# Attention moved whole ahead of the first MLP, in blocks of 32 queries by 38 keys, with a fixed TensorE order and weights kept on chip

## The chip, the core and the metric

One core of a Trainium2 chip runs the whole program. The engines are TensorE (PE; its weight loads are PEld), VectorE (DVE), ScalarE (ACT), GpSimd (POOL) and SyncE (SP), which here issues all DMAs. The metric is the device time of one execution in microseconds (us), lower is better, and the median of several runs is compared.

## What is computed

Attention of 2 batches, 8 heads, 576 positions and head size 64, a gated MLP (512 to 2048 to 512) and a dense MLP of four experts (512 to 1024 to 512), all in float32. Cut to what matters:

```python
out_d = sm_attn(q_d, k_d, v_d)             # q, k, v averaged over 4 neighbours: 144 positions
out_up = np.repeat(out_d, 4, axis=2)
mask = np.abs(pos[:, None] - pos[None, :]) < 4      # 7 keys for each query
attn = softmax(np.where(mask, scores, -1e9))
x = out_up + attn @ v                      # -> 1152 tokens x 512
h = x @ w_in                               # 512 x 2048, float64 in memory
g = h * np.clip(h + 3.0, 0.0, 6.0) / 6.0
x = g @ w_out                              # 2048 x 512, float64 in memory
for e in range(4):
    out += p[:, e:e+1] * (np.maximum(x @ w1[e], 0.0) @ w2[e])
```

## The kernel before

**MLP products.** Each float32 product runs as three float32r passes (function `three`, L246 to L248): every operand is split into a high and a low part, and high*high, high*low and low*high are added up in PSUM. So weights are needed as split tiles `whl` of 128 x 2 x 1024.

**Conversion.** The first MLP's weights are 16 float64 tiles (8 of `w_in`, even numbers; 8 of `w_out`, odd ones). The generator `converting()` turns each into float32 `cm` and splits it. For one tile DVE runs one L166 (mantissa), two L177 (low words), one L188 (power of two) and two L202 (product); ACT runs two L146 and two L155 (high part), and POOL two L156 (low part). Each `yield` is a step; the code that emits the kernel takes steps between other work. The float32 tile is also written to a DRAM buffer `kept` (L159).

**First MLP.** Tokens go in three blocks of 512, 352 and 288 (`BLOCKS`). For each of 16 pieces f of the hidden size `first(b, f)` makes 12 matmuls into PSUM `ps`, ACT (L584) and DVE (L586) make the gate `u`, ACT (L558) and DVE (L559) split it into `g`, and two pieces later `second(b, f)` makes 12 matmuls into the accumulators `acc`. `first` for an even f needs tile f, `second` tile f+1. For blocks 2 and 3 all 16 tiles are read back from `kept` and split again: DVE L227 copies the high part, DVE or POOL (L231) subtracts.

**Attention.** A pair of heads (128 partitions) and a chunk of 288 positions make three groups: each head's local part, in 3 tiles of 96 queries by 104 keys, and both heads' pooled part. A group goes through `scores` (L386 mask, L395 or L405 products, L414 maximum, L417), `exps` (L426, one ACT instruction for each tile, with its sum), `norm` (L438, L447, and POOL L448), `turn` (L463 transposes, L469 copy) and `values` (L481, L492, L500, L502, L510, L512: the split `x`). The local products use all 128 rows of the array, with zeros in the other head's half of `qz`. Chunks 0 and 1 stand ahead of the first MLP, chunk 2 is emitted between the pieces of block 1, chunk 3 between those of block 2.

**Order.** Each engine runs its own instructions in a fixed order and waits on semaphores. The code is written in emission order; a scheduler of the framework then orders each engine's list, TensorE's too.

**Second MLP.** For each expert and 384 tokens, `first2` (8 pieces of 12 matmuls of 384 columns; L655, L656 split) and then the second product (L778 to L780, 512 columns, L790).

Of the kernel before, what the change touches and what calls it, by code (L numbers as in the profile page):

```python
# [17 lines left out]
F32 = mybir.dt.float32  # L18
# [58 lines left out]
def model(ctx: ExitStack, tc: tile.TileContext, qT, kT, v, dp, w_in, w_out, w1, w2, out):  # L77
    nc = tc.nc
    const = ctx.enter_context(tc.tile_pool(name="const", bufs=1))
    big = ctx.enter_context(tc.tile_pool(name="big", bufs=1))  # L80
    rawp = ctx.enter_context(tc.tile_pool(name="raw", bufs=3))
    wa_p = ctx.enter_context(tc.tile_pool(name="wa", bufs=NWA))
    dram = ctx.enter_context(tc.tile_pool(name="kept", bufs=1, space=bass.MemoryType.DRAM))
    acc_p = ctx.enter_context(tc.tile_pool(name="accp", bufs=1, space=PSUM))
    mm_p = ctx.enter_context(tc.tile_pool(name="mm", bufs=2, space=PSUM))
    early_p = tc.alloc_tile_pool(name="early", bufs=1)
    att = tc.alloc_tile_pool(name="att", bufs=1, side="right")
    cv_p = tc.alloc_tile_pool(name="cv", bufs=2, side="right")
    sc_p = tc.alloc_tile_pool(name="sc", bufs=1, space=PSUM)

    products = [mm_p]

    def product():
        products.append(products.pop(0))
        return products[-1].tile([P, 512], F32, tag="mm", name="ps")

    def wide(i):
        return acc_p.tile([P, 512], F32, tag=f"acc{i}", name=f"acc{i}")

    EARLY = [lambda: sc_p.tile([P, 512], F32, tag="sc", name="sc")]  # L100
    EARLY += [lambda i=i: wide(i) for i in (0, 1, 3)]
    EARLY += [lambda: sc_p.tile([P, 512], F32, tag="tr", name="tr"), lambda: wide(2)]
    EARLY += [product]
# [5 lines left out]
    kept = [dram.tile([P, 2, WT], F32, name=f"kept{i}") for i in range(NW1 // 2)]  # L109
# [3 lines left out]
    for _ in BLOCKS[1:]:  # L113
        sources += [k.rearrange("p a n -> p (a n)") for k in kept]
# [4 lines left out]
    # Split tiles by number: 16 of the first MLP for each block, then 8 for each expert.  # L119
    first_e = NW1 * len(BLOCKS)  # L120
# [8 lines left out]
    def converting():  # L129
        """Rounds UP times the float64 tiles to float32, splits and keeps them. Yields at each step.  # L130

        The top 16 bits of a float64, as if they were a bfloat16, are a number whose exponent and
        mantissa hold float64's exponent. As a float16 they have its lower 8 bits, in float32's
        bias, where a bfloat16 has its exponent, so without the mantissa that is the power of two
        (tiny numbers vanish, huge ones saturate; REBIAS moves the range). It multiplies the
        mantissa, which is its upper 20 bits with the leading one, plus the low word over 2**32,
        and so 2**20 times what it stands for.
        """
# [11 lines left out]
        def put(i):  # L150
            f = m_t.pop(i)
            whl[i] = wa_p.tile([P, 2, WT], F32R, tag="w", name="whl")
# [10 lines left out]
        for i in range(NW1):  # L163
# [32 lines left out]
            if i:  # L196
                while i - 1 - NWA > used[0]:
                    yield True
                put(i - 1)
# [5 lines left out]
        while NW1 - 1 - NWA > used[0]:  # L205
            yield True
# [5 lines left out]
    split = [NW1]  # L212

    def split_to(n):
        """Splits up to tile n: the float32 tiles, after the converted ones."""
        while n >= 0 and n < NW1 and n not in whl and next(conv, 0) is None:
            pass
        while split[0] <= min(n, first_e + 8 * E - 1):
            i = split[0]
            j = NW1 + (i - NW1) // 2  # L220
            load_to(j)
            pool = pools["w1"] if i >= first_e and (i - first_e) % 8 < 4 else wa_p
            t = pool.tile([P, 2, WT], F32R, tag="w", name="whl")
            src = raw[j][:, (i % 2) * WT : (i % 2 + 1) * WT]
            for s in HALVES:
                if i < first_e:
                    nc.vector.tensor_copy(t[:, 0, s], src[:, s])  # L227
                else:
                    nc.scalar.activation(out=t[:, 0, s], in_=src[:, s], func=AF.Copy)  # L229
                eng = nc.gpsimd if i < first_e and i % 2 else nc.vector  # L230
                eng.tensor_tensor(  # L231
                    out=t[:, 1, s], in0=src[:, s], in1=r32(t[:, 0, s]), op=ALU.subtract
                )
            whl[i] = t
            split[0] += 1
            if i % 2:
                raw.pop(j)
                load_to(j + 3)

    pools = {}  # L240
# [10 lines left out]
    NQB = 5  # L251
    qz = [att.tile([P, 2, CH], F32, name=f"qz{i}") for i in range(NQB)]
    q_t, k_t, vw_t, vd_t, qd_t, kd_t = {}, {}, {}, {}, {}, {}

    def load_q(j):
        c, hp = divmod(j, NHP)
        b, s = divmod(c, 2)
        t = qz[j % NQB]
        nc.sync.dma_start(out=t[0:D, 0], in_=qT[b, s, 0:D, hp])
        nc.sync.dma_start(out=t[D:P, 1], in_=qT[b, s, D:P, hp])  # L260
        q_t[c, hp] = t

    def load_k(b, hp):
        t = att.tile([P, S], F32, tag="k", name="k", bufs=NHP)
        nc.sync.dma_start(out=t, in_=kT[b, :, hp])
        k_t[b, hp] = t

    def window(c, i):
        q0 = (c % 2) * CH + i * QT
        return min(max(q0 - (FACTOR - 1), 0), S - W)  # L270

    def load_v(c):
        for i in range(NQ):
            ks = window(c, i)
            t = att.tile([W, DM], F32, tag=f"vw{i}", name=f"vw{i}", bufs=2)
            nc.sync.dma_start(out=t, in_=v[c // 2, ks : ks + W, :])
            vw_t[c, i] = t
# [4 lines left out]
    vr_t = {}  # L282

    def load_vpool(b):
        for kc in range(2):
            t = wa_p.tile([P, 2, WT], F32R, tag="w", name="vr")
            t = r32(t[:KC]).rearrange("p a (r d) -> p (a r) d", r=2)
            nc.sync.dma_start(
                out=t,
                in_=v[b, kc * KC * FACTOR : (kc + 1) * KC * FACTOR, :].rearrange(  # L290
                    "(p r) d -> p r d", r=FACTOR
                ),
            )
            vr_t[b, kc] = t

    def pool_v(b, eng):
        vd_t[b] = att.tile([KC, 2, DM], F32, tag="vd", name="vd")
        for kc in range(2):
            t = vr_t.pop((b, kc))
            for r in range(2):  # L300
                add(eng, t[:, r], t[:, r], t[:, r + 2])
            add(eng, vd_t[b][:, kc], t[:, 0], t[:, 1])

    def sum4(src, n, tag, eng):
        """Sums of four neighbours of src [P, 4n]."""
        t = att.tile([P, n], F32, tag=tag, name=tag, bufs=NHP if tag == "kd" else 2)
# [4 lines left out]
        half = att.tile([P, n, 2], F32, tag="half", name="half", bufs=2)  # L311
# [5 lines left out]
    for i in range(4):  # L317
        load_k(0, i)
        load_q(i)
        if i == 1:  # L320
            load_v(0)
        if i == 2:
            load_vpool(0)
    load_q(NHP)
    load_v(1)
    warm = const.tile([P, 1], F32, name="warm")
    nc.vector.memset(warm, 0.0)
# [30 lines left out]
    class Group:  # L358
# [112 lines left out]
        def values(self):  # L471
            """Products with v, of the pair's three groups together."""
            aT_t[self.kind] = self.aT
            if self.kind < 2:
                return
# [375 lines left out]
```

## Time and profile before

| | |
|---|---|
| median of 3 runs | 745.77 us (745.34 to 747.49) |
| span of the profiled execution, first to last instruction | 741.5 us |
| busy: PE, PEld, DVE, ACT, POOL | 688.2, 619.5, 399.6, 243.3, 187.1 us |
| first product of MLP 1, first of MLP 2, last matmul | at 63.6, 334.4 and 738.1 us |

The profiled execution has only its span; the device time of a run has 4.3 us more around it (745.77 - 741.5). Instructions on PE are pipelined, so a busy PE is no proof of full speed.

### The profile page before, as it was taken

The numbers are of one execution on the slowest core, as the hardware profiler recorded it, in microseconds if no ns is written. First come the engines' busy times: TensorE is split into PE (matmuls) and PEld (weight loads), VectorE is DVE, ScalarE is ACT, GpSimd is POOL, SyncE is SP. The second block draws the span as 40 slices with busy tenths as digits, with TensorE's granted clock in tenths as the row PEclk, the third lists the DMA queues.
The fourth block names the chain that finished last, engine by engine and source line by source line (L and its number), as shares of the span: only waits on it lengthen the run. The fifth ranks groups of instructions, "written<-read, shape, count | busy, mean of one in ns | idle before, by whom it ended". The sixth has DMA issues, their size and how long they took to land.

```text
span 741.5 us, 10241 instructions
## 1 busy us (share of the span) xinstructions
PE 688.2 (93%) x3960; PEld 619.5 (84%) x3960; DVE 399.6 (54%) x754; ACT 243.3 (33%) x670; POOL 187.1 (25%) x163
## 2 busy tenths in 40 slices
PE   4967977788999899999999999999999999999998
PEld 4855765566898889989898989989898989989897
DVE  6998999999777768895121442223341223322121
ACT  3785545653343433264020431103230112201020
POOL 2688497795345344410000000000000000000000
PEclk9997998999999999999999999999999999999999
DMA  7855865565332233464000311001130000000001
GB/s 184 274 177 169 238 242 173 203 224 174 114 114 66 106 114 114 171 242 156 0 1 1 114 57 57 1 1 57 57 114 1 0 1 1 0 15 29 30 15 43
DMA packets 16301, 71.40 MB, mean 96 GB/s; under 512 B 2172, under 2 KB 4476, under 8 KB 9820
## 3 DMA queue, kind: packets, MB, share of 16 engines
q1 hardware_dynamic: 16252, 70.74, 28.6%
q8 instruction: 31, 0.51, 0.3%
q14 instruction: 18, 0.15, 0.1%
HBM read 59.98 MB, written 10.75 MB: 95 GB/s over the span
## 4 chain that ended last, share of the span: by engine, by line
PE 69%; DVE 20%; issue 3%; ACT 3%; DMA 2%; POOL 1%; SPq 1%; ACTq 0%; POOLq 0%; DVEq 0%
PE ps L246 11%; PE ps L247 11%; PE ps L248 11%; PE acc L780 9%; PE acc L779 9%; PE acc L778 9%; DVE cm L177 3%; DVE whl L227 2%; PE acc L246 2%; DVE cm L202 2%; PE acc L247 2%; PE acc L248 2%; DVE den L438 2%; ACT ex L426 2%; DVE g L559 2%
## 5 line engine op out<-in xcount | busy, mean ns | idle before, releaser
L246 PE MATMUL ps<-x,whl 128*128 128x384 f32 (+3 forms) x576 | 198.7, 345 | 3.8 <-DVE xf L502 2.6
L248 PE MATMUL ps<-x,whl 128*128 128x384 f32 (+3 forms) x576 | 196.7, 341 | 0.0
L247 PE MATMUL ps<-x,whl 128*128 128x384 f32 (+3 forms) x576 | 196.4, 341 | 0.0
L655 ACT ACTIVATE h<-ps 128x384 fp32r<-128x384 f32 x96 | 47.1, 491 | 271.0 <-PE ps L248 270.9
L656 DVE SCALAR_TENSOR_TENSOR h<-ps,h 128x384 fp32r<-128x384 f32 x96 | 53.5, 557 | 127.5 <-ACT h L655 127.5
L246 PEld LDWEIGHTS ps<-x,whl 128*128 128x128 f32 x576 | 109.2, 189 | 7.8 <-DVE xf L502 3.1
L780 PE MATMUL acc<-whl,h 128*128 128x512 f32 (+1 forms) x296 | 113.8, 385 | 0.0
L779 PE MATMUL acc<-whl,h 128*128 128x512 f32 (+1 forms) x296 | 113.7, 384 | 0.0
L778 PE MATMUL acc<-whl,h 128*128 128x512 f32 (+1 forms) x296 | 113.5, 383 | 0.0
L247 PEld LDWEIGHTS ps<-x,whl 128*128 128x128 f32 x576 | 109.2, 190 | 3.2 <-POOL x L512 0.2
L248 PEld LDWEIGHTS ps<-x,whl 128*128 128x128 f32 x576 | 109.1, 189 | 2.8
L231 DVE TENSOR_TENSOR whl<-raw,whl 128x512 fp32r<-128x512 f32 x96 | 65.4, 710 | 13.7 <-ACT whl L229 13.3
L448 POOL TENSOR_TENSOR ex<-ex,rec 96x312 f32<-96x312 f32 (+1 forms) x48 | 54.7, 1142 | 47.0 <-DVE rec L447 20.8
L246 PE MATMUL acc<-g,whl 128*128 128x512 f32 (+2 forms) x192 | 65.8, 343 | 0.3 <-ACT g L558 0.3
L247 PE MATMUL acc<-g,whl 128*128 128x512 f32 (+2 forms) x192 | 64.7, 337 | 1.4 <-DVE g L559 1.4
L780 PEld LDWEIGHTS acc<-whl,h 128*128 128x128 f32 x296 | 55.6, 188 | 11.0
L779 PEld LDWEIGHTS acc<-whl,h 128*128 128x128 f32 x296 | 55.6, 188 | 10.8
L248 PE MATMUL acc<-g,whl 128*128 128x512 f32 (+2 forms) x192 | 64.6, 337 | 0.0
L778 PEld LDWEIGHTS acc<-whl,h 128*128 128x128 f32 x296 | 55.6, 188 | 10.7
L231 POOL TENSOR_TENSOR whl<-raw,whl 128x512 fp32r<-128x512 f32 x32 | 44.8, 1413 | 56.5 <-DVE whl L227 21.3
L156 POOL TENSOR_TENSOR whl<-cm,whl 128x512 fp32r<-128x512 f32 x32 | 47.5, 1496 | 23.3 <-ACT whl L155 20.4
L790 DVE SCALAR_TENSOR_TENSOR acc<-acc,pr,acc 128x512 f32<-128x512 f32 x18 | 13.5, 751 | 73.6 <-PE acc L780 73.6
(88 smaller groups left out, 864.3 us busy)
## 6 DMA issues: line engine op xcount, KB each, us to landing
raw<-kept SPq DMA_DIRECT2D x16, 1024.0 KB
raw<-in_w_dram SPq DMA_DIRECT2D x16, 1024.0 KB
raw<-in_w_in_dram SPq DMA_DIRECT2D x8, 1024.0 KB
raw<-in_w_out_dram SPq DMA_DIRECT2D x8, 1024.0 KB
kept<-cm SPq DMA_DIRECT2D x16, 512.0 KB
vw<-in_v_dram SPq DMA_DIRECT2D x12, 208.0 KB
k<-in_kT_dram SPq DMA_DIRECT2D x8, 288.0 KB
qz<-in_qT_dram SPq DMA_DIRECT2D x32, 72.0 KB
```

What stands on the lines that cost most here:

```text
L156: nc.gpsimd.tensor_tensor(out=whl[i][:, 1, s], in0=f[:, s], in1=r32(hi), op=ALU.subtract)
L177: nc.vector.scalar_tensor_tensor(out=m[:, s], in0=words[:, s, 0].bitcast(U32), scalar=2.0**-32, in1=m[:, s].bitcast(I32), op0=ALU.mult, op ...
L231: eng.tensor_tensor(out=t[:, 1, s], in0=src[:, s], in1=r32(t[:, 0, s]), op=ALU.subtract)
L246: nc.tensor.matmul(ps, wh, xh, start=first, stop=False)
L247: nc.tensor.matmul(ps, wh, xl, start=False, stop=False)
L248: nc.tensor.matmul(ps, wl, xh, start=False, stop=last)
L448: nc.gpsimd.tensor_tensor(out=self.ex, in0=self.ex, in1=rec.unsqueeze(2).to_broadcast([R, n, C]), op=ALU.mult,)
L655: nc.scalar.activation(out=h[:, 0, :], in_=ps, func=AF.Relu)
L656: nc.vector.scalar_tensor_tensor(out=h[:, 1, :], in0=ps, scalar=0.0, in1=r32(h[:, 0, :]), op0=ALU.max, op1=ALU.subtract,)
L778: nc.tensor.matmul(ps, hh, w[:, 0], start=(f == 0), stop=False)
L779: nc.tensor.matmul(ps, hh, w[:, 1], start=False, stop=False)
L780: nc.tensor.matmul(ps, hl, w[:, 0], start=False, stop=(f == NF2 - 1))
```

## The change

All eight pairs of heads (units of 576 queries) are now worked through before the first MLP, one unit in each turn of a loop, with `values` two turns and `turn` one turn behind. The local part is cut into 18 blocks of 32 queries by 38 keys. Three blocks j share a 96-partition tile, the two heads h use the two halves of the array's rows, and the results of a unit's two heads fill two PSUM banks, so that one instruction of DVE, ACT or POOL works on 456 columns of 96 partitions. A block's transposed weights of 38 keys lie at partition 0 or 64, and a value product is 38 rows by 64 columns with 32 moving columns. TensorE is taken out of the scheduler (`manual_schedule`): its list is the emission order. Split tiles 4 to 11 of the first MLP stay on chip, the other 8 are split again once (from `kept`), block 2 goes through the pieces backwards, and POOL splits only in the conversion.

```diff
+QB = 32
+NJ = 3
+QT = NJ * QB
+W = QB + 2 * (FACTOR - 1)
+NA, NB = 4, 8
...
+    ctx.enter_context(tc.manual_schedule(engines={mybir.EngineType.PE}))
...
+    def stays(n):
+        return NA <= n < NA + NB
...
-            nc.sync.dma_start(out=kept[i // 2][:, i % 2, :], in_=f)
+            if not stays(i):
+                nc.sync.dma_start(out=kept[i // 2][:, i % 2, :], in_=f)
...
+        def scores(self):
+            q, k = q_t[self.u], k_t[self.u]
+            for i in range(NI):
+                for j in range(NJ):
+                    q0, ks = i * QT + j * QB, window(i, j)
+                    for h in range(2):
+                        d = slice(h * D, (h + 1) * D)
+                        nc.tensor.matmul(
+                            self.sc[j * QB : (j + 1) * QB, h, i * W : (i + 1) * W],
+                            q[d, q0 : q0 + QB],
+                            k[d, ks : ks + W],
...
+        def values(self):
...
+                            nc.tensor.matmul(
+                                pv[h * D : (h + 1) * D, r, c0 : c0 + QB],
+                                vw[keys, p, j, col[h] : col[h] + D],
+                                self.aT[keys, h, c0 : c0 + QB],
...
+        pieces += [(b, f) for f in (reversed(fs) if b % 2 else fs)]
...
+    for t in range(NU + 2):
+        if t < NU:
+            n = units[t]
+            n.sums()
+            n.masks()
+            n.scores()
+            n.pooled_scores()
+            n.softmax()
+            n.pooled_softmax()
...
+        if t >= 2:
+            units[t - 2].values()
+        if 1 <= t <= NU:
+            units[t - 1].turn()
+            units[t - 1].pooled_turn()
...
+        if t >= 5:
+            step(conv, 3)
+    ps_a.release()
...
+    mlp1(0, lambda slot: step(conv, 3))
```

`units[u].softmax()` is, on DVE, the maximum and its subtraction from PSUM (now L401, L403), a sum (L412) and its reciprocal; on ACT one exponential (L410); on POOL the product with the reciprocal (L418). `pooled_softmax()` is as before (L452, L454, four exponentials L464, L473, L478), of 576 columns. The conversion's lines are now L146, L155, L156, L167, L178, L189 and L203, the gate's L591, L592, L557 and L558. `banks()` hands out four pairs of PSUM banks in rotation, five in each turn.

On TensorE, after the sixth unit's scores, the list of the changed kernel reads as follows (`ps` are the pairs of banks; L373 masks, L388 local scores, L440 pooled scores, L511 and L520 values, L427 and L491 transposes):

```order
L388 MATMUL ps_1135<-k,q 32x38 x36
L440 MATMUL ps_1174<-kd,qd 72x144 x4
L511 MATMUL ps_1204<-aT,vw 64x32 x36
L520 MATMUL ps_1204<-aTd,vd 64x144 x4
L427 MATMUL ps_1252<-ident,ex_160 128x96 x6
L491 MATMUL ps_1261<-ident,exd 72x72 x8
L511 MATMUL ps_1288<-aT,vw 64x32 x36
L520 MATMUL ps_1288<-aTd,vd 64x144 x4
```

In the kernel before, at block 1 of the first MLP, it reads:

```order
L246 MATMUL ps<-x,whl 128x512
L247 MATMUL ps<-x,whl 128x512
L386 LDWEIGHTS identb
L386 MATMUL sc<-mask_177,identb 96x312
L395 MATMUL sc<-k,qz_96 96x104 x3
L248 MATMUL ps<-x,whl 128x512
L463 MATMUL tr<-ident,ex 104x96 x3
```

Attention no longer stands between the products of the first MLP; products of an MLP come after the last unit's values only.

On VectorE the first conversions of the changed kernel stand behind the sixth unit's split `x` (L543); xf (L532) is a unit's sum of its two value products:

```order
L412 TENSOR_REDUCE sm<-ex_161 96x12
L454 TENSOR_SCALAR nm<-mxd 72x4
L413 TENSOR_SCALAR sm<-sm 96x12
L532 TENSOR_TENSOR xf<-ps_1204,pd 128x3x96
L417 RECIPROCAL rec<-sm 96x12
L532 TENSOR_TENSOR xf<-ps_1204,pd 128x3x96
L473 TENSOR_SCALAR den<-smd 72x4
L477 RECIPROCAL recd<-den 72x4
L543 TENSOR_TENSOR x<-xf,x 128x576
L167 TENSOR_SCALAR cm<-raw 128x1024
L178 SCALAR_TENSOR_TENSOR cm<-raw,cm 128x512 x2
L189 TENSOR_SCALAR cg<-cg 128x1024
```

In the kernel before, conversions stand among the groups of chunk 1:

```order
L166 TENSOR_SCALAR cm<-raw 128x1024
L447 RECIPROCAL rec<-den 72x2
L438 TENSOR_SCALAR den<-sm 96x3
L177 SCALAR_TENSOR_TENSOR cm<-raw,cm 128x512
L502 TENSOR_TENSOR xf<-ps,pd 128x288
L447 RECIPROCAL rec<-den 96x3
L414 TENSOR_REDUCE mx<-acc_804 96x3
```

So none of the 16 tiles is begun on VectorE before the sixth unit is done.

The end of the conversion on VectorE in the changed kernel (t is the gate, of pieces 8 and 9 here; g the split gate, of pieces 8 and 9 in the row x2):

```order
L558 TENSOR_TENSOR g<-t,g 128x512
L178 SCALAR_TENSOR_TENSOR cm<-raw,cm 128x512 x2
L592 SCALAR_TENSOR_TENSOR t<-t,ps 128x512
L189 TENSOR_SCALAR cg<-cg 128x1024
L592 SCALAR_TENSOR_TENSOR t<-t,ps 128x512
L203 TENSOR_TENSOR cm<-cm,cg 128x512 x2
L558 TENSOR_TENSOR g<-t,g 128x512 x2
```

Tile 15 is converted (L203) ahead of the split gates of pieces 8 to 15; the first row is that of piece 7.

## Rows read from the trace of the kernel before

**Rows 1.** The page: span, and busy tenths in 40 equal slices.

```profile
span 741.5 us, 10241 instructions
DVE  6998999999777768895121442223341223322121
POOL 2688497795345344410000000000000000000000
```

**Rows 2.** Stretches: their length, each engine's busy us (instructions), granted TensorE clock, DMA.

```profile
62.00:175.00 113.00, 89.27 (x479) 69.29 (x480) 110.42 (x162) 64.07 (x166) 84.17 (x57) 0.94 0.60 199
175.00:207.00 32.00, 32.00 (x169) 27.51 (x166) 25.73 (x42) 11.30 (x25) 15.83 (x14) 1.00 0.41 139
207.00:288.00 81.00, 75.49 (x557) 72.55 (x556) 58.39 (x129) 33.78 (x114) 33.96 (x33) 1.00 0.30 105
288.00:342.00 54.00, 52.31 (x385) 51.87 (x384) 44.75 (x80) 22.69 (x49) 15.16 (x11) 1.00 0.54 195
342.00:738.00 396.00, 396.00 (x2016) 362.44 (x2014) 109.74 (x181) 72.15 (x145) 0.00 (x0) 1.00 0.09 30
```

**Rows 3.** VectorE in order of time, from 168.3 us: start, length, line, instruction.

```profile
168.34 0.68 DVE L166 TENSOR_SCALAR cm<-raw 128x1024 int32<-128x1024 int32 x1
168.95 1.50 DVE L188 TENSOR_SCALAR cg<-cg 128x1024 uint16<-128x1024 uint16 x1
170.37 2.40 DVE L177 SCALAR_TENSOR_TENSOR cm<-raw,cm 128x512 f32<-128x512 uint32 x2
172.69 0.67 DVE L586 SCALAR_TENSOR_TENSOR u<-t,ps 128x512 f32<-128x512 f32 x1
173.28 1.28 DVE L202 TENSOR_TENSOR cm<-cm,cg 128x512 f32<-128x512 f32 x2
174.49 0.68 DVE L559 TENSOR_TENSOR g<-u,g 128x512 fp32r<-128x512 f32 x1
```

**Rows 4.** GpSimd in order of time, the same stretch.

```profile
168.56 3.05 POOL L156 TENSOR_TENSOR whl<-cm,whl 128x512 fp32r<-128x512 f32 x2 [1.30 <-ACT whl L155]
```

**Rows 5.** TensorE in order of time, two stretches of attention's products.

```profile
25.56 0.41 PE L463 MATMUL acc<-ident,ex 72*72 72x72 f32 x4
...
174.92 0.23 PE L492 MATMUL tr<-aT,vd 72*64 72x72 f32 x1
...
175.11 0.45 PE L492 MATMUL tr<-aT,vd 72*64 72x72 f32 x5
```

**Rows 6.** The start: VectorE, then TensorE.

```profile
6.93 0.66 DVE L355 COPY mask<-mf 96x104 bf16<-96x104 bf16 x6
...
7.57 1.24 PE L395 MATMUL sc<-k,qz 128*96 128x104 f32 x6
```

**Rows 7.** Attention's other operations by line and shape: busy us, mean ns of one.

```profile
L426 ACT ACTIVATE ex<-sc,nm 72x144 f32<-72x144 f32 x20 | 7.4, 374 | 13.7 <-DVE nm L417 10.6 <-DVE rec L447 2.1 <-PE ps L248 0.9
...
L414 DVE TENSOR_REDUCE mx<-sc 96x3 f32<-96x312 f32 x20 | 9.4, 470 | 2.2 <-PE sc L395 2.2
...
L469 ACT ACTIVATE aT<-tr 104x288 f32<-104x288 f32 x24 | 9.8, 407 | 2.4 <-PE tr L463 2.0
...
L502 DVE TENSOR_TENSOR xf<-tr,pd 128x288 f32<-128x288 f32 x8 | 3.6, 447 | 0.3 <-ACT pd L500 0.3
```

**Rows 8.** TensorE in order of time, products of the MLPs with 512, 352 and 288 columns.

```profile
458.75 0.39 PE L778 MATMUL acc<-whl,h 128*128 128x512 f32 x1
...
459.88 0.39 PE L780 MATMUL acc<-whl,h 128*128 128x512 f32 x1
...
209.91 0.32 PE L247 MATMUL ps<-x,whl 128*128 128x352 f32 x1
...
212.95 0.32 PE L248 MATMUL acc<-g,whl 128*128 128x352 f32 x1
...
295.86 0.30 PE L248 MATMUL acc<-g,whl 128*128 128x288 f32 x1
...
296.92 0.29 PE L247 MATMUL acc<-g,whl 128*128 128x288 f32 x1
```

More of the change, by code (lines that the diff above doesn't have):

```diff
@@ L211, in model, with split_next @@
     conv = converting()
[L212 to L240, printed above, removed]
+    split = [0]
+    def split_next():
+        if split[0] == len(order):
+            return
+        i = split[0]
+        key, j = order[i], NW1 + i // 2
+        load_to(j)
+        t = pool_of(key).tile([P, 2, WT], F32R, tag="w", name="whl")
+        src = raw[j][:, (i % 2) * WT : (i % 2 + 1) * WT]
+        for s in HALVES:
+            nc.scalar.activation(out=t[:, 0, s], in_=src[:, s], func=AF.Copy)
+            nc.vector.tensor_tensor(
+                out=t[:, 1, s], in0=src[:, s], in1=r32(t[:, 0, s]), op=ALU.subtract
+            )
+        whl[key] = t
+        split[0] += 1
+        if i % 2:
+            raw.pop(j)
+            load_to(j + 3)
     def three(ps, wt, cols, x_hl, first, last):
@@ L268, in window, with load_qk @@
[L268 to L277, printed above, removed]
+    q_t, k_t, vw_t, vr_t, vd_t = {}, {}, {}, {}, {}
+    def load_qk(u):
+        b, hp = divmod(u, NHP)
+        k_t[u] = att.tile([P, S], F32, tag="k", name="k", bufs=NHP)
+        nc.sync.dma_start(out=k_t[u], in_=kT[b, :, hp])
+        q_t[u] = att.tile([P, S], F32, tag="q", name="q", bufs=NHP)
+        nc.sync.dma_start(
+            out=q_t[u].rearrange("p (s c) -> p s c", s=2),
+            in_=qT[b, :, :, hp, :].rearrange("s p c -> p s c"),
+        )
@@ new lines, in window, with load_v @@
+    def window(i, j):
+        return min(max(i * QT + j * QB - (FACTOR - 1), 0), S - W)
+    def load_v(b, g):
+        n = DM // 2
+        t = att.tile([P, NI // 2, NJ, n], F32, tag="vw", name="vw", bufs=3)
+        for i in range(NI):
+            r, p = i % 2, i // 2
+            runs = [[0]]
+            for j in range(1, NJ):
+                if window(i, j) - window(i, j - 1) == QB:
+                    runs[-1].append(j)
+                else:
+                    runs.append([j])
+            for run in runs:
+                src = v[b, window(i, run[0]) : window(i, run[0]) + W, g * n : (g + 1) * n]
+                (row, _), (one, _) = src.ap
+                nc.sync.dma_start(
+                    out=t[r * WP : r * WP + W, p, run[0] : run[-1] + 1, :],
+                    in_=bass.AP(
+                        src.tensor, src.offset, [[row, W], [QB * row, len(run)], [one, n]]
+                    ),
+                )
+        vw_t[b, g] = t
@@ L314, in sum4 @@
         return t
[L317 to L325, printed above, removed]
+    load_qk(0)
+    load_qk(1)
+    load_v(0, 0)
+    load_qk(2)
+    load_vpool(0, 0)
+    load_qk(3)
+    load_v(0, 1)
     warm = const.tile([P, 1], F32, name="warm")
@@ new lines, in turn @@
+        def turn(self):
+            tr = banks()
+            for h in range(2):
+                for p in range(NI // 2):
+                    nc.tensor.transpose(
+                        tr[:, h, p * QT : (p + 1) * QT],
+                        self.ex[:, h, 2 * p : 2 * p + 2, :].rearrange("q r w -> q (r w)"),
+                        ident[:QT, :QT],
+                    )
+            self.aT = att.tile([P, 2, NI // 2 * QT], F32, tag="aT", name="aT", bufs=2)
+            nc.scalar.activation(out=self.aT, in_=tr[:, :, : NI // 2 * QT], func=AF.Copy)
@@ L409, in scores, with pooled_scores @@
+        def pooled_scores(self):
+            self.sd = banks()
+            for qh in range(2):
+                for h in range(2):
+                    d = slice(h * D, (h + 1) * D)
+                    nc.tensor.matmul(
+                        self.sd[:KC, h, qh * PK : (qh + 1) * PK],
+                        self.qd[d, qh * KC : (qh + 1) * KC],
+                        self.kd[d],
                         start=True,
@@ L561, in finish_g, with need @@
         )
+    def need(n, b):
+        if b == 0:
+            while n not in whl and next(conv, 0) is None:
+                pass
+        else:
+            while n not in whl:
+                split_next()
     def first(b, f):
         start, n_tok = BLOCKS[b]
-        n = b * NW1 + f // 2 * 2
-        split_to(n)
+        n = f // 2 * 2
+        need(n, b)
         w4 = whl[n].rearrange("p a (k n) -> p a k n", k=KD)
```

574 lines of the change are left out of this document (244 added, 330 removed).

## The prediction

> **What bounds the kernel now.** I first read the slices of the page [rows 1]: VectorE is at nine tenths up to slice 11, some 200 us, and GpSimd works over the same slices; afterwards both are nearly free. The table of stretches [rows 2] then gives three regimes. From 342 us on TensorE has no gap, 396.00 of 396.00 us: the second MLP, which the change leaves alone. From 207 to 342 us (blocks 2 and 3 of the first MLP, with chunk 3) TensorE is close to full, but its 12 products a piece share it with attention. From 62 to 175 us VectorE is busy for 110.42 of 113 us, TensorE for 89.27, at a clock of 0.94: here VectorE is waited for. What it does there I read in order of time [rows 3, 4]. L188 takes 1.50 us where its work is 0.35: it ends at 170.45, and a GpSimd L156 had started at 168.56. GpSimd's second L156 then ends at 171.61 (168.56 + 3.05), and the two L177, in the row from 170.37, end at 172.77, 1.16 us after it, which is what two of them need. VectorE's conversion and GpSimd's subtraction thus run one after the other, never together; the gate u, which reads PSUM, takes its plain 0.67.
>
> [...]
>
> **The price of a conversion.** By the starts in [rows 3], one L166 is 0.60 us, L188 0.34, two L177 1.20, two L202 1.20: 3.34 us of VectorE for a tile. GpSimd's two are 1.25 each, 2.50. [...]
>
> **The change, step by step.** The profiled execution has a span of 741.5 us, 4.3 below the median, and I build the new span from its start.
>
> *a. Start.* The last mask copy ends at 7.6 us [rows 6], and the new masks need much the same. The first passes run at half clock: 104 columns in 0.173 us ((1.24 - 0.38)/5) [rows 6]. I put the end of unit 0's scores at 12 us, unit 1's at 17. VectorE's list has unit 1's maximum ahead of unit 0's reciprocal, so GpSimd scales unit 0 at 18 and its pooled part at 20.7; transposes follow, and unit 2's scores end at 24.
>
> *b. Small products.* A float32 product is two passes in the trace (3 in a list, 6 in a row). Alone, a pass of 72 columns takes 0.06 us ((0.41 - 0.23)/3) [rows 5], 0.83 ns a column, so 38 columns would be 32 ns. Passes into different halves of the array's columns already run together: from 174.92 to 175.11 us five start, 38 ns each, though one alone is 60 or 80 [rows 5]. No row shows 38 or 32 columns, nor the halves of the rows. Bounds: 17 ns (32 shared by two) and 62 ns (the nearest row, one at a time). I take 35, just under the 38 seen, because the pieces are shorter and up to six parts of the array are in use. A unit's 72 passes of scores are then 2.5 us, its 72 of values 2.5.
>
> [...]
>
> *c. A turn.* On TensorE: masks 0.25, scores 2.5, pooled scores 0.75, values 3.1, transposes 1.0: 7.6 us. But the next turn's masks take the banks that the four pooled exponentials read. From the end of the scores VectorE needs 0.62 for the maximum and 0.62 for its subtraction (470 ns for 312 columns [rows 7], here 456), 0.75 for the pooled maximum, 0.61 for the sum, 0.15 for nm; then ScalarE 4 x 0.42 (374 ns and its sum's reading) [rows 7], and some 0.1 from one to the next: 4.9 us. Where ScalarE's list has pd of the unit two back ahead of the exponentials (units 2, 5 and 7; for unit 4 the 0.64 us copy aT too, twice the 407 ns [rows 7]), they start only when the values are done. Five turns come to 8.8, 7.8, 9.7, 8.8 and 7.8 us, 42.9 together: unit 7's scores end at 67. VectorE's own work in a turn is some 5.5 us (xf two of 447 ns [rows 7]), GpSimd's 3.3: neither binds. Nothing converts meanwhile, since the conversion stands behind unit 5's split x. That x is 7.5 us after unit 7's scores (pooled scores and values 3.9, exponentials, high part and x 3.6): the conversion starts at **74.5 us**. Bounds by b: 64 and 95.
>
> *d. Conversion to the last L203.* 16 tiles x 5.84 = 93.4, less tile 15's subtractions, which come later, 2.5: 90.9. Eight split gates ahead of it: 4.8. The x of units 6 and 7: 1.3. GpSimd's last pooled product: 1.2. Ten gates from PSUM, half beside GpSimd: 3. Sums xf: 1. VectorE idle while unit 6's values are late: 2. Four `kept` copies that a later tile's buffer waits for: 1. Together **105 us** (bounds 93, if two or three tiles of subtractions lag behind and the last four terms vanish, and 112, if the copies stall it): the last L203 at 179.5.
>
> *e. What is left of block 1 then.* TensorE's list has second(8) after first(10), and g of piece 8 stands behind the last L203. So TensorE, with 51.7 us of products since about 86 us, stands waiting; it still has eight second and five first, 13 x 12 products at 0.227 us [rows 8], 35.4, after 1.2 us for g: **36.6 us**, to 216. Before, block 1 ended at 207 [rows 2]; so far the change loses 9.
>
> *f. Blocks 2 and 3.* Twice 192 products of 352 columns at 0.160 us ((212.95 - 209.91)/19) and of 288 at 0.1325 ((296.92 - 295.86)/8) [rows 8]: 61.4 + 50.9 us. Attention is gone from them, and eight splits instead of 32 leave VectorE room. At two block ends the accumulators must be read first: 3 us. **115.3 us**, to 331.5; before, 81 + 54 less the 4.2 us of the two pieces of MLP 2 in it [rows 2], to 338.
>
> *g. The second MLP*, with the 4.2 us: 400.2 us, and 3.4 from the last matmul to the span's end, as before: 403.6.
>
> Sum: 74.5 + 105 + 36.6 + 115.3 + 403.6 = 735.0 us, 6.5 less than 741.5. Median: **739.3 us**.
>
> The weights kept on chip I cost at nothing in DMA: stretches past 175 us move at most 195 GB/s with 0.54 of the DMA engines busy [rows 2], and TensorE's work covers it; without that cover a tile of 1 MB would be some 5 us.
>
> **The rivals.**
> 1. *As summed:* 739 us, itself 728 to 751. Chance 0.50.
> 2. *Small products overlap well and subtractions lag:* passes at 25 ns, between 17 and 35, take 10 ns x 144 off each of about seven turns, 8 to 10 us counting the start, and three tiles' subtractions after the last L203 another 5: about 726. For it: the 38 ns of [rows 5] is what two halves of the array's columns allow at 72 and 96 columns (31 and 41), so no limit of issue shows in it. Against: the chain in c, not TensorE, sets two of five turns. Chance 0.18.
> 3. *One small product at a time* (the other side): at 62 ns scores and values are 4.5 us each, a turn over 11, the conversion starts at 95: 760, slower. Each ns costs about 1.05 us, so it decides from 41 ns on. For it: masks, scores, values and transposes use the array's rows and columns in different parts by turns, and no row shows passes that short. Against: five passes at 38 ns on average. Chance 0.22.
> 4. *VectorE and GpSimd do not hold each other up:* the conversion is VectorE's 3.34 alone, it keeps ahead, and block 1 is TensorE's 87.2 us from 86 us: 86 + 87.2 + 115.3 + 403.6 = 692, median 697. Against: [rows 3, 4]. Chance 0.04.
> 5. *Nothing measurable:* what blocks 2 and 3 win is what block 1 loses, 745 us. For it: 9 of the 16 us won are already given back. Chance 0.06.
>
> **How the numbers follow.** 0.3% of the median, 2.2 us, is about what a measurement of this kernel can tell from no change: faster is below 743.5, slower above 748.0. Of case 1 some 0.34 lie below, 0.10 between, 0.06 above. Faster: 0.34 + 0.18 + 0.04 = 0.56. Same: 0.10 + 0.06 = 0.16. Slower: 0.06 + 0.22 = 0.28. The likeliest case's own range is 728 to 751; for 8 in 10 it must reach to cases 2 and 3: 716 to 764.
>
> **What would show it.** a to c: the first L167 on VectorE at about 74 us (64 to 95) with unit 7's scores ending 7 us earlier, and passes of L388 and L511 35 ns apart. d: the last L203 some 105 us later, with L156 and L167, L178, L189 never together. e: TensorE waiting for g (L558) with pieces 8 to 15 still open, and block 1's last product near 216. f: blocks 2 and 3 at 0.16 and 0.13 us a product without gaps, the second MLP's first product near 328. The prediction is wrong if the conversion ends well before 170 or the turn is over 10 us, or if blocks 2 and 3 hold waits that I left out.

## The result, and the profile after

The changed kernel takes 756.31 us (median of 4 runs, 754.74 to 757.00) against 745.56 (median of 4) of the kernel before: 1.0149 times as long, with a 95% interval of 1.0124 to 1.0173. It is slower by 1.5%. I had forecast 739.3 and a gain. The profiled execution has a span of 754.7 us, where my sum gave 735.0. Its device time is 756.47, 1.8 us more than its span, and the runs below have 1.7 to 1.9 as well; my 4.3 us were such 1.8, and 2.5 by which the profiled execution of the kernel before lay below its median.

The page of the changed kernel, beside [rows 1]:

```profile
span 754.7 us, 10848 instructions
PE   2585748667799999999999999999999999999998
DVE  3674469999724423666121442123341214112121
POOL 3434524856300000000000000000000000000000
DMA  3344367646400300343000122000310000000001
GB/s 120 100 124 120 116 220 230 229 167 219 171 1 0 112 1 1 104 175 132 37 1 1 56 95 74 1 0 1 112 56 0 1 1 1 0 15 29 28 15 43
```

The first five slices (94 us) are attention. VectorE, which I expected to be ready for the conversion at 74.5 us, is at 3 to 7 tenths there, TensorE at 2 to 8, and the DMA engines move 100 to 124 GB/s at 3 to 4 tenths. No engine is full, so something is waited for. SP's queue in order of time says what (start, length over the instructions of the row, line; L274 loads windows of v, L249 and L251 k and q, L286 v for pooling, L126 raw weights):

```profile
0.75 0.38 SPq L249 DMA_DIRECT2D k<-in_kT_dram  x1
1.19 0.42 SPq L251 DMA_DIRECT2D q<-in_qT_dram  x1
1.65 0.47 SPq L249 DMA_DIRECT2D k<-in_kT_dram  x1
2.16 0.43 SPq L251 DMA_DIRECT2D q<-in_qT_dram  x1
2.64 12.52 SPq L274 DMA_DIRECT2D vw<-in_v_dram  x8
15.20 1.00 SPq L249 DMA_DIRECT2D k<-in_kT_dram  x1
16.25 0.43 SPq L251 DMA_DIRECT2D q<-in_qT_dram  x1
...
21.94 15.25 SPq L274 DMA_DIRECT2D vw<-in_v_dram  x8
...
44.42 15.23 SPq L274 DMA_DIRECT2D vw<-in_v_dram  x8
...
77.53 11.87 SPq L274 DMA_DIRECT2D vw<-in_v_dram  x7
89.44 0.57 SPq L126 DMA_DIRECT2D raw<-in_w_in_dram  x1
```

Eight window loads hold the queue for 12.5 to 15.3 us, where four loads of k and q went out in 1.8, and there are four such groups (the last one as a single load and, behind a wait, seven in 11.9 us). Unit 2's k and q stand behind the first, the raw weights behind the last. Stretches in which mostly window loads run (length, each engine's busy us, granted clock, share of the DMA engines, GB/s; for the 1.00 of the clock see **b** further down):

```profile
7.00:14.00 7.00, 5.28 (x164) 3.83 (x163) 4.19 (x10) 1.48 (x6) 1.43 (x3) 1.00 0.14 49
28.00:36.00 8.00, 6.98 (x172) 5.70 (x171) 6.67 (x16) 3.32 (x11) 4.96 (x6) 1.00 0.15 50
51.00:58.00 7.00, 7.00 (x115) 5.86 (x121) 5.55 (x14) 2.84 (x9) 3.91 (x4) 1.00 0.14 48
81.00:88.00 7.00, 7.00 (x181) 5.63 (x178) 4.18 (x9) 3.03 (x7) 4.80 (x4) 1.00 0.14 48
```

48 to 50 GB/s at 0.14 to 0.15: as much as 2.2 to 2.4 of the sixteen DMA engines would have if they were busy all the time, an estimate (0.14 and 0.15 x 16). The first row of VectorE's conversion names what it waited for:

```profile
100.14 0.69 DVE L167 TENSOR_SCALAR cm<-raw 128x1024 int32<-128x1024 int32 x1 [8.59 <-DMA raw<-in_w_in_dram]
```

The conversion starts at 100.1 us, when the first raw tile has landed, 25.6 after my 74.5. Of this, 8.6 are that last wait. The other 17 lie in attention itself: unit 2's scores end at 31.6 us in place of 24, those of units 4 and 6 wait 3.1 and 6.8 us for their q, and unit 5's split x is done at 91.6. From there on the trace differs little from my sum:

| term, us | predicted | changed kernel | 48 rows a load | changed, TensorE's order free |
|---|---|---|---|---|
| a to c: to the first L167 | 74.5 | 100.1 | 70.3 | 100.6 |
| d: to the last L203's end | 105 | 98.4 | 100.9 | 98.4 |
| e: to block 1's last product | 36.6 | 42.8 | 41.8 | 35.8 |
| f, g: to the span's end | 518.9 | 513.4 | 513.4 | 513.4 |
| span | 735.0 | 754.7 | 726.4 | 748.2 |

The last two columns are experiments below.

### The profile page after: what moved, and what is told of

The parts are those of the page before. It is cut to its first block, busy times and chain, and to the rows that moved or that the text cites. A ratio compares the mean times of both kernels' runs of the same rounds, so it can differ in the third digit from the quotient of the medians.

```text
span 754.7 us, 10848 instructions
## 1 busy us (share of the span) xinstructions
PE 677.4 (90%) x4600; PEld 608.9 (81%) x4600; DVE 322.4 (43%) x537; ACT 217.8 (29%) x454; POOL 97.3 (13%) x84
## 4 chain that ended last, share of the span: by engine, by line
PE 77%; DVE 8%; DMA 6%; SPq 4%; POOL 3%; issue 2%; ACT 1%; DVEq 0%; POOLq 0%; ACTq 0%
PE ps L239 12%; PE ps L240 12%; PE ps L241 12%; PE acc L783 9%; PE acc L781 9%; PE acc L782 9%; PE acc L240 4%; PE acc L241 4%; PE acc L239 4%; SPq L274 3%; DVE cm L178 3%; DMA q<-in_qT_dram 2%; DVE cg L189 1%; DMA raw<-in_w_in_dram 1%; DVE cm L203 1%
## 5 line engine op out<-in xcount | busy, mean ns | idle before, releaser
L239 PE MATMUL ps<-x,whl 128*128 128x384 f32 (+3 forms) x576 | 195.7, 340 | 10.2 <-DVE xf L532 10.2
L240 PE MATMUL ps<-x,whl 128*128 128x384 f32 (+3 forms) x576 | 195.0, 339 | 0.0
L241 PE MATMUL ps<-x,whl 128*128 128x384 f32 (+3 forms) x576 | 194.8, 338 | 0.0
L239 PEld LDWEIGHTS ps<-x,whl 128*128 128x128 f32 x576 | 109.2, 190 | 14.3 <-issue 10.7
L240 PE MATMUL acc<-g,whl 128*128 128x512 f32 (+2 forms) x192 | 68.4, 356 | 20.5 <-DVE g L558 20.5
L791 DVE SCALAR_TENSOR_TENSOR acc<-acc,pr,acc 128x512 f32<-128x512 f32 (+1 forms) x28 | 20.5, 731 | 118.7 <-PE acc L783 118.7
L239 PE MATMUL acc<-g,whl 128*128 128x512 f32 (+2 forms) x192 | 66.9, 348 | 0.7 <-ACT g L557 0.7
L241 PE MATMUL acc<-g,whl 128*128 128x512 f32 (+2 forms) x192 | 67.4, 351 | 0.0
L783 PEld LDWEIGHTS acc<-whl,h 128*128 128x128 f32 x296 | 55.7, 188 | 12.1
L156 POOL TENSOR_TENSOR whl<-cm,whl 128x512 fp32r<-128x512 f32 x32 | 57.1, 1799 | 52.4 <-ACT whl L155 52.2
L240 PEld LDWEIGHTS acc<-g,whl 128*128 128x128 f32 x192 | 37.6, 196 | 25.8 <-DVE g L558 22.9
L226 DVE TENSOR_TENSOR whl<-raw,whl 128x512 fp32r<-128x512 f32 x80 | 51.8, 687 | 3.9 <-ACT whl L225 2.9
L592 DVE SCALAR_TENSOR_TENSOR t<-t,ps 128x512 f32<-128x512 f32 (+2 forms) x48 | 26.3, 550 | 63.5 <-ACT t L591 63.5
```

The lines of the kernel that those rows point to most:

```text
L156: nc.gpsimd.tensor_tensor(out=whl[i][:, 1, s], in0=f[:, s], in1=r32(hi), op=ALU.subtract)
L226: nc.vector.tensor_tensor(out=t[:, 1, s], in0=src[:, s], in1=r32(t[:, 0, s]), op=ALU.subtract)
L239: nc.tensor.matmul(ps, wh, xh, start=first, stop=False)
L240: nc.tensor.matmul(ps, wh, xl, start=False, stop=False)
L241: nc.tensor.matmul(ps, wl, xh, start=False, stop=last)
L592: nc.vector.scalar_tensor_tensor(out=t, in0=t, scalar=1.0, in1=ps, op0=ALU.min, op1=ALU.mult)
```

## The experiments

**Theory L:** a window load covers 38 partitions, and few DMA engines work on such a load. **Rival N:** the number of loads, or their pieces of 1 KB, is the cost. **Rival O:** only their place on the queue. **Rival P:** TensorE's fixed order and attention's own chain set the start.

All results (`first L167` is the conversion's start, `last L203` its end but for the last tile's halves, `block 1` its last product; ratio to the kernel before, with its 95% interval):

| run | us | ratio | first L167 | last L203 | block 1 |
|---|---|---|---|---|---|
| kernel before | 745.56 | 1 | 33.0 | 174.6 | 204.9 |
| changed kernel | 756.31 | 1.0149 (1.0124 to 1.0173) | 100.1 | 198.5 | 241.3 |
| 48 rows | 731.55 | 0.9805 (0.976 to 0.985) | 70.3 | 171.2 | 213.0 |
| 40 rows | 730.68 | 0.9804 (0.9764 to 0.9844) | 71.3 | 172.4 | 215.5 |
| q and k first | 757.64 | 1.0166 (1.0125 to 1.0207) | 100.7 | 200.3 | 242.2 |
| 37 rows, one run | 810.91 | none | 155.2 | 253.3 | 295.7 |
| 32 + 6 rows | 739.64 | 0.9917 (0.9891 to 0.9943) | 87.8 | 183.1 | 225.3 |
| low halves on VectorE | 743.49 | 0.9971 (0.9949 to 0.9994) | 101.1 | 186.7 | 228.3 |
| changed, free order | 750.06 | 1.0054 (1.003 to 1.0079) | 100.6 | 199.0 | 234.8 |
| 48 rows, free order | 724.14 | 0.9712 (0.9666 to 0.9758) | 72.1 | 173.3 | 209.0 |
| 48 rows, low | 717.87 | 0.9618 (0.959 to 0.9646) | 72.5 | 161.6 | 203.0 |
| 48 rows, early | 736.47 | 0.9876 (0.9839 to 0.9913) | 40.2 | 173.5 | 221.5 |
| 48 rows, low, early | 726.73 | 0.9737 (0.9708 to 0.9766) | 39.9 | 165.1 | 212.1 |
| 48 rows, low, v sums | 715.02 | 0.9595 (0.9551 to 0.9639) | 71.0 | 158.4 | 199.6 |
| sum of the gains | 712.60 | 0.9558 (0.9515 to 0.9601) | 71.5 | 161.3 | 195.7 |
| sum, early | 717.53 | 0.9615 (0.9593 to 0.9637) | 57.5 | 161.8 | 201.5 |
| before, low | 727.06 | 0.9759 (0.9709 to 0.9809) | 33.2 | 166.2 | 187.7 |

### The rows of a load

48 rows, and the same with 40:

```diff
+                R = 48 if window(i, run[-1]) + 48 <= S else W
-                src = v[b, window(i, run[0]) : window(i, run[0]) + W, g * n : (g + 1) * n]
+                src = v[b, window(i, run[0]) : window(i, run[0]) + R, g * n : (g + 1) * n]
-                    out=t[r * WP : r * WP + W, p, run[0] : run[-1] + 1, :],
+                    out=t[r * WP : r * WP + R, p, run[0] : run[-1] + 1, :],
```

> The changed kernel, with 48 rows of v in each window's load in place of 38 (two of 24 pieces, at the sequence's end, stay at 38; the ten rows more are never read). 26% more bytes, as many loads, the same order. Theory L (the window loads are slow because a load over 38 partitions is worked by few DMA engines: eight of them take 15.2 us at 46 to 53 GB/s with 0.11 to 0.14 of the engines busy, and q, k and the first raw weights stand behind them on SP): eight loads take 3 to 5 us, unit 2's scores start near 14 us in place of 30.6, the first L167 near 70 to 76 in place of 100.1, and the time falls by 24 to 30 us, to 726 to 732. [...] Rival N (it is the number of loads, or pieces of 1 KB): no gain, 756 to 760. Rival P (TensorE's fixed order and attention's own chain set the start, the loads are only late beside it): the loads end sooner, the first L167 stays past 92, 748 or more.

> As the run with 48 rows, but with 40 rows in each window's load (5% more bytes than 38). [...] Rival N: no change, 754 to 757. Rival P: 748 or more.

37 rows (and 37 keys in the product with v):

```diff
+                R = 37
```

> The changed kernel with 37 rows of v in each window's load, so that the last key of each window is left out of the values. 3% fewer bytes than 38, the same number of loads. [...] Rival N (number of loads, pieces of 1 KB): no change, 752 to 757. Rival M (too few bytes, or rows not a multiple of 8 or 16, give one slow speed): 752 to 760.

In the runs with 48 and 40 rows one of the eight loads of a group, that of the last window, stays at 38 (the "two of 24 pieces" of the expectation are a miscount). The first groups of SP's queue, and a later stretch in which hardly anything but window loads runs, with 48 rows:

```profile
2.65 5.20 SPq L275 DMA_DIRECT2D vw<-in_v_dram  x8
...
11.70 9.32 SPq L275 DMA_DIRECT2D vw<-in_v_dram  x8
```

```profile
58.00:60.00 2.00, 2.00 (x21) 1.54 (x18) 0.64 (x3) 1.47 (x9) 0.95 (x1) 0.50 1.00 227
```

With 40 rows:

```profile
2.63 5.07 SPq L275 DMA_DIRECT2D vw<-in_v_dram  x8
```

```profile
30.00:32.00 2.00, 2.00 (x68) 1.93 (x66) 1.97 (x6) 0.64 (x2) 0.00 (x0) 0.50 0.66 212
```

With 37 rows:

```profile
2.64 26.35 SPq L275 DMA_DIRECT2D vw<-in_v_dram  x8
...
35.49 29.74 SPq L275 DMA_DIRECT2D vw<-in_v_dram  x8
```

```profile
45.00:62.00 17.00, 13.58 (x355) 11.20 (x352) 10.19 (x23) 9.41 (x34) 5.48 (x6) 0.70 0.08 26
82.00:98.00 16.00, 12.17 (x224) 10.11 (x220) 8.50 (x23) 8.01 (x26) 4.79 (x5) 0.50 0.08 25
```

By L I had expected 728 to 736 us for 40 rows and 795 to 825 for 37; they take 730.68 and 810.91. One row less halves the rate (25 GB/s, share 0.08) and doubles the group (29.7 us); two rows more end the standstill (212 GB/s, share 0.66). The bytes go the other way and the number of loads stays, so the rows of a load set its rate: L holds in this, and N falls; M falls too, since 37 and 38 rows differ. The shares of 0.08, 0.14, 0.66 and 1.00 for 37, 38, 40 and 48 rows are as much as 1.3, 2.2, 10.6 and 16 of the sixteen engines busy all the time, an estimate; how many engines work on a load, and why, was not shown. The rates of 25, 50 and 212 GB/s are as 1 to 2 to 8.5; 48 rows, at 227, move hardly more than 40, which fits the equal times of the two runs. What holds the rate there is not shown. The 24.8 us that 48 rows win are the whole loss and 14 us more. P as a cause of the late start falls too: with fast loads the first L167 stands at 70.3 us, right behind unit 5's split x, where the prediction had put it.

### The place and the number of the loads

```diff
-    load_qk(0)
-    load_qk(1)
-    load_v(0, 0)
-    load_qk(2)
-    load_vpool(0, 0)
-    load_qk(3)
-    load_v(0, 1)
+    for u in range(NHP):
+        load_qk(u)
+    load_vpool(0, 0)
+    load_v(0, 0)
+    load_v(0, 1)
```

> The changed kernel with its loads as they are (38 rows), but q and k of units 0 to 3 and the pooled v stand ahead of all v windows on SP. Theory L: unit 2's scores start near 14 in place of 30.6, but the four window loads still take about 15 us each, the values of unit 0 wait for the first of them until about 29, and the first raw weights still land behind the last one: first L167 at 92 to 101, the time 748 to 757. Rival O (only the order is at fault: q and k behind windows that are needed later): first L167 at 74 to 82, 730 to 738.

Unit 2's scores start at 23.3 us in place of 30.6, and nothing comes of it: the sixteen windows then take one row of 29.8 us, and the raw weights still land at 100. O falls.

```diff
+                for a, z in ((0, 32), (32, W)):
+                    ...
+                    out=t[r * WP + a : r * WP + z, p, run[0] : run[-1] + 1, :],
```

> The changed kernel with each window's load cut in two, 32 rows and 6: the same bytes in the same pieces, and twice as many loads (64 in place of 32). [...] Rival N (the number of loads sets it): the loads take up to twice as long, 756 or more. Rival B (the ten rows more of the other run helped by something else than engines, such as bytes in a piece): 752 to 757.

Twice the loads and the same bytes are faster by over 2%, so N falls for good, and B with it; the first sixteen take 7.91 us. The time lies 3 us above the 728 to 737 that I expected by L. On the queue the last group goes out at 65.5 us in place of the 55.4 of the run with 48 rows, and the raw weights follow it. In both runs the load of pooled v ahead of it stands behind GpSimd (14.3 and 12.1 us), but here GpSimd begins the sums that it waits for at 60.1 us in place of 48.5, since attention's turns come later. Why they do was not followed up.

### The conversion's price

```diff
-                nc.gpsimd.tensor_tensor(
+                nc.vector.tensor_tensor(
                     out=whl[i][:, 1, s], in0=f[:, s], in1=r32(hi), op=ALU.subtract
                 )
```

> The changed kernel, with the low halves of the converted weights subtracted on VectorE in place of GpSimd (one word changed). My price of a conversion (VectorE's 3.34 us and GpSimd's 2.50 never run together): a tile takes 3.34 + 2 x 0.60 = 4.54 us in place of 5.84, the stretch from the first L167 to the last L203 falls from 98 to 75 to 80 us, the time by 16 to 22, to 734 to 740. Rival (GpSimd's share mostly lay beside VectorE's work): VectorE gets 19 us more to do, the stretch grows to 105 to 117, 763 to 775.

> 48 rows in the window loads, and the low halves on VectorE. If the conversion still ends what TensorE waits for, the 12.6 us by which the stretch from the first L167 to the last L203 shrank with the low halves alone come off again: 716 to 721. Rival: once the loads are fast, the inputs of units 6 and 7 and TensorE's first products bind, and the low halves on VectorE win under 5 us: 727 or more.

> The kernel before, with the low halves of the converted weights on VectorE in place of GpSimd and nothing else. VectorE bounds its block 1 too (110.42 of 113 us), and GpSimd's subtractions there do not run beside VectorE's work: 8 to 13 us faster, as this edit won 12 and 14 us in the changed kernel: 733 to 738. Rival: in the kernel before the subtractions lie under other waits of VectorE (attention's), and the edit wins under 3 us: 743 to 747.

The stretch from the first L167 to the last L203 falls from 98.4 to 85.6 us; VectorE takes on 32 operations more and is done sooner. So GpSimd's subtractions do hold VectorE up. But I had all 2.50 us of GpSimd's in the price, which less VectorE's 1.20 would have won 20.8 us over 16 tiles, and 12.8 came: some of GpSimd's time lay beside VectorE's after all, or behind its end (in the changed kernel three L203 pairs follow each other within 6.4 us, ending at 136.9, 139.9 and 143.3, with the subtractions left for later). In the kernel before the same edit wins 18 us, more than I expected; its last L203 ends 8.4 us sooner and its block 1 17.2.

### TensorE's order

```diff
-    ctx.enter_context(tc.manual_schedule(engines={mybir.EngineType.PE}))
```

> 48 rows in the window loads, and TensorE's order left to the scheduler (the line that fixes it is out). If the fixed order is no part of the loss: 728 to 735, as with 48 rows. Rival P (the fixed order costs something in attention or block 1): 718 to 726. If the order that the scheduler picks is worse, 738 or more, and the fixed order is worth that much to the change.

> The changed kernel (38 rows) with TensorE's order left to the scheduler, nothing else. If the fixed order leaves more of block 1 behind the last conversion (167 products and two waits of 1.8 us, where the free order left 138 with the 48 rows): 4 to 7 us less, 749 to 753. Rival (the slow loads give TensorE time, so that the order does not matter here): 755 to 758.

Both win, 7.4 and 6.2 us by the medians (4.0 and 6.5 in the spans), so P holds for block 1: the fixed order, a part of the change, costs about as much as that. In both e is the term that falls, from 41.8 and 42.8 to 35.7 and 35.8. TensorE of the changed kernel around the last L203 (198.5) and at block 1's end; the bracket is idle time and what ended it:

```profile
193.59 0.79 PE L240 MATMUL acc<-g,whl 128*128 128x512 f32 x1 [5.39 <-DVE g L558]
...
198.02 0.63 PE L241 MATMUL acc<-g,whl 128*128 128x512 f32 x1
198.44 0.59 PE L239 MATMUL ps<-x,whl 128*128 128x512 f32 x1
...
231.46 0.39 PE L241 MATMUL acc<-g,whl 128*128 128x512 f32 x1
231.69 0.32 PE L239 MATMUL ps<-x,whl 128*128 128x352 f32 x1
```

While weights are still converted, the fixed order keeps TensorE waiting for g, although first products of later pieces have their weights. So 167 products of block 1 start after the last L203 (the free order leaves 138; 29 x 0.227 us is 6.6). In the expectations I read two gaps of 1.8 us near the end as waits; they are no waits, as the row from 231.69 shows: first pieces of block 2 stand there.

### Starting the conversion earlier, and the sum

```diff
+        if t == 1:
+            load_to(2)
-        if t >= 5:
+        if 2 <= t <= 8:
             step(conv, 3)
```

> 48 rows in the window loads, and three steps of the conversion behind each turn from the third to the ninth on VectorE's, ScalarE's and GpSimd's lists (in place of from the sixth on), the first three raw tiles loaded behind unit 5's q. Theory: while attention runs, VectorE stands idle for 15 of the 58 us from 14 to 72; the conversion fills some of it, starts at 32 to 45, and the last L203 comes 5 to 12 us sooner: 718 to 727. Rival: each step of the conversion delays attention's softmax by its own length, the last unit's x comes later by what the conversion won, and the time stays within 3 us of the 48 rows alone, 728 to 735.

> All three: 48 rows, low halves on VectorE, conversion from the third turn on. If the gains add: 705 to 716. Rival: the early conversion wins nothing, and the time is that of 48 rows with the low halves on VectorE, within 3 us.

Both miss: the conversion starts at 40 us and the time is 5 and 9 us worse than without. SP's waits from 20 to 100 us (for what, us in total, times, longest) in the run with 48 rows:

```profile
SPq L126 <- DVE cm L178: 23.4, 2, 18.5
SPq L287 <- POOL vd L296: 18.1, 1, 18.1
```

The last load of pooled v waits for GpSimd's sums of the one before (20.7 us in the run with the low halves on VectorE; 12.1 and 14.6 in the same two kernels without the early conversion), and behind that load on SP stand unit 7's k and q and the last windows: unit 7's scores start at 76.6 in place of 61.8. So I gave VectorE those sums:

```diff
-            pool_v(1, t // 4, nc.gpsimd)
+            pool_v(1, t // 4, nc.vector)
```

> 48 rows, low halves on VectorE, and the pooled sums of v of the second half of the batch on VectorE in place of GpSimd. In the run without this the sums stand on GpSimd's list until 55.8 us, unit 7's pooled scores wait for GpSimd behind them until 57, and SP waits with the next load of pooled v and seven window loads from 39.7 to 55.8. If that delays units 6 and 7: 711 to 715. Rival: the conversion still ends last whatever units 6 and 7 do: 716 to 720, as without it.

> 48 rows, low halves and the second half's pooled sums of v on VectorE, and TensorE's order free: if the gains add, 707 to 711. Rival: with a shorter conversion less of block 1 is left to reorder, and the time is 713 to 717, as with the fixed order.

> As the run with the sum of the gains, with the first three raw tiles loaded behind unit 6's q and three steps of the conversion a turn from the fifth turn on (one turn sooner). If the early conversion lost before because SP stood behind the pooled sums on GpSimd, which is not so here: the first L167 at 45 to 62, the time 2 to 8 us below that of the sum. Rival (each step delays attention's own work by its length): the same time within 2 us, or above it.

The sums on VectorE win 2.9 us by the medians, but the executions overlap (714.13 to 717.73 against 716.26 to 718.40). The sum of the gains is the fastest kernel here, 712.60 (0.9558 of before), though above the 707 to 711 expected, just below its rival's 713, and its gain over the fixed order, 2.4 by the medians, is not certain (710.25 to 716.91 against 714.13 to 717.73). The early conversion loses again, now without the wait for GpSimd: SP's longest wait for the pooled v is 12.3 us, behind VectorE, and 12.5 in the sum itself. TensorE in that run, at unit 7, and then GpSimd:

```profile
65.01 1.07 PE L388 MATMUL ps<-k,q 64*32 64x38 f32 x72 [2.54 <-DMA q<-in_qT_dram]
75.19 1.24 PE L440 MATMUL ps<-kd,qd 64*72 64x144 f32 x8 [9.11 <-POOL qd L295]
```

```profile
66.41 6.74 POOL L478 TENSOR_TENSOR exd<-exd,recd 72x576 f32<-72x576 f32 x1 [3.02 <-DVE recd L477]
```

Unit 7's pooled scores wait 9.11 us for GpSimd, which itself stood 15.1 us behind VectorE's reciprocals in that stretch (55 to 90 us) and took 6.74 us for one product that mostly takes 1.14: the conversion delays the softmax it shares VectorE with. The rival holds there.

## Why the prediction was wrong

**What failed** is the step from c to "the conversion starts at 74.5 us". It builds attention from the engines' work, and the loads of attention have no price in it. My only words on DMA were for the kept weights. The kernel's text showed loads of 38 partitions in place of 104 and 32 of them, and I counted neither. They cost 24.8 us by the medians, and turn a gain into a loss. (In the spans it is 28.3, but the profiled execution with 48 rows was the fastest of its four, 728.21 us.) With them mended, the median is 731.55, 7.8 below my 739.3.

**b, the small products,** was mis-sized twice, and by luck the two errors nearly cancel. TensorE in the changed kernel, units 2, 4 and 5 (a unit has 72 passes):

```profile
30.56 1.08 PE L388 MATMUL ps<-k,q 64*32 64x38 f32 x72
31.57 1.24 PE L440 MATMUL ps<-kd,qd 64*72 64x144 f32 x8
```

```profile
78.14 2.14 PE L511 MATMUL ps<-aT,vw 38*64 38x32 f32 x72
80.21 1.23 PE L520 MATMUL ps<-aTd,vd 72*64 72x144 f32 x8
81.37 1.22 PE L427 MATMUL ps<-ident,ex 96*128 96x96 f32 x6
...
86.04 1.31 PE L511 MATMUL ps<-aT,vw 38*64 38x32 f32 x72
87.28 0.71 PE L520 MATMUL ps<-aTd,vd 72*64 72x144 f32 x8
87.92 0.71 PE L427 MATMUL ps<-ident,ex 96*128 96x96 f32 x6
```

By the starts, scores are 14 ns a pass (1.01 us for 72), values 29 (2.07) and from 86.04 us on 17 (1.24), where I had 35 and a lower bound of 17. So the passes overlap much better than I took them to.

The other way went the clock. From 86 us on the pooled products and the transposes, too, take little over half of what the same rows took before: lengths of 0.71 for 1.23 and for 1.22. The run with 48 rows shows both levels beside their granted clock, 0.50 and 1.00:

```profile
25.00:33.00 8.00, 8.00 (x178) 6.78 (x178) 6.92 (x16) 5.08 (x19) 2.98 (x3) 0.50 0.97 254
39.00:47.00 8.00, 5.72 (x186) 4.82 (x185) 5.63 (x17) 4.76 (x17) 2.97 (x2) 1.00 0.49 150
```

```profile
29.24 2.14 PE L512 MATMUL ps<-aT,vw 38*64 38x32 f32 x72
...
40.84 0.84 PE L389 MATMUL ps<-k,q 64*32 64x38 f32 x72
41.61 0.71 PE L441 MATMUL ps<-kd,qd 64*72 64x144 f32 x8
```

At 0.50 values take the same 2.07 us, at 1.00 scores take 0.77, 11 ns a pass. In the changed kernel, too, values from 102.14 us on take 2.08 us by the starts, at a granted clock of 0.50. So, by the lengths, its attention ran at half clock up to 86 us; the 1.00 in its stretches is no measurement, as that trace records the clock only from 86 us on. I had priced all turns but the first passes at full clock. By the starts the pooled products take 1.17 and 1.16 us and the transposes 1.02 and 0.95, which I had at 0.75, 0.6 and 1.0 together, so the turn came out near the 7.8 us of my shortest: with 48 rows the scores of units 2 to 4 follow each other by 7.9 us, with TensorE busy all the time (8.00 of 8.00 us), so that there TensorE sets the turn and not the chain in c. The gain below 35 ns was rival 2's ground; the clock took it away. No profiled run here has all of attention at the full clock.

**d** was 6.6 us too long (98.4 for 105): its 5.84 us a tile put VectorE's 3.34 and GpSimd's 2.50 [rows 3, 4] wholly one after the other. No run shows that the two never work together: by this price the low halves on VectorE would have won 20.8 us, and they won 12.8, so it was too strict by about 8. (A split gate's 0.60 us is VectorE's step from 174.49 us [rows 3] to its next instruction at 175.09. In [rows 3] only L166 and L202 can be read by the starts; L188 and L177 stand there with their waits, 1.42 and 2.32 us. The prices of 0.34 and 1.20 hold all the same: the changed kernel's first tile, with GpSimd idle, has 0.33 and 1.22.) **e** was 6.2 too short. Of this 3.8 us (24 products of block 2 at 0.160, which I had counted in f) only stand elsewhere. The other 2.5 us are 11 products more than the 156 counted: 71 first products were open, some six pieces and not five. **f and g** are 5.5 too long, of which 3.8 are those same 24 products; the rest I put down to the 3 us for reading accumulators, since TensorE has no idle time in these stretches of the changed kernel:

```profile
242.00:302.00 60.00, 60.00 (x383) 60.00 (x382) 22.47 (x43) 21.30 (x42) 0.00 (x0) 1.00 0.11 36
302.00:354.00 52.00, 52.00 (x386) 52.00 (x386) 33.35 (x67) 30.69 (x66) 0.00 (x0) 1.00 0.41 142
```

So the gain in blocks 2 and 3 is there, and the kept weights do cost nothing. It is even larger than I had it. Block 1 of the kernel before ends at 204.9 us and not at 207, where I had only cut a stretch of [rows 2]:

```profile
204.47 0.39 PE L248 MATMUL acc<-g,whl 128*128 128x512 f32 x1
205.31 0.41 PE L246 MATMUL ps<-x,whl 128*128 128x352 f32 x1
```

From block 1's last product to the span's end it is 536.6 us before and 513.4 after, 23.2 less (I had 16), and block 1 ends 36.4 us later (I had 9): together the 13.2 us between the spans.

**Rival 3** named 760 us and a late conversion, but by products at 62 ns; its number was near by luck, its cause is refuted. (Its figures don't agree with each other either: 27 ns at 1.05 us each are 28 us, not the 21 from 739 to 760.) What the change would be worth with fast loads and the free order is 724.14, of the same size as the 0.9759 that one word wins in the kernel before.

Still open is what part each other piece of the change has in the 14 us that 48 rows win over the kernel before; it wasn't taken apart.

## What to carry to other kernels

Look at the partition count of every load that a change brings in, not at its bytes: the DMA share of a stretch, 0.14 with 38 rows where 48 had 1.00, tells at a glance. Two rows of padding were enough here: 40 did as well as 48 (730.68 and 731.55 us). A slow load, or one that waits for a buffer, was paid here by everything behind it on SP's queue, q, k and the weights of the next stage: the first conversion started at 100.1 us in place of the 70.3 with 48 rows. And when a stage is moved ahead of another, its loads belong into the sum with its instructions.

## What the runs showed of the hardware

- One row halved the rate of the window loads, and two more raised it to four times: 37 rows 25 to 26 GB/s, 38 rows 48 to 50, 40 rows 212, 48 rows 227. From 40 to 48 rows the rate hardly grew.
- Passes into different parts of TensorE's array overlap far more than I thought: 64 rows by 32 columns of the array, 38 columns long, start 14 ns apart in the changed kernel, by its lengths at half clock, and 11 with 48 rows at a granted clock of 1.00 (21 ns for the two passes of a product), where I took 35.
- TensorE ran most of attention at half of its clock: with 48 rows the granted clock was 0.50 from 25 to 33 us and 1.00 from 39 to 47, and in the changed kernel the values of units 0 to 4 had a length of 2.14 us each, those of unit 5, from 86 us on, one of 1.31.
- Moving a subtraction from GpSimd to the busier VectorE won 13 us in the changed kernel, 14 with 48 rows and 18 in the kernel before: here GpSimd's share cost VectorE more than doing the work itself.
